# One store instead of two for the last rows, and a cast cut along another dimension, in a fused attention and mixer kernel

## The chip, the cores and the metric

The kernel runs on one core of one Trainium2 chip. The metric is the device time of one execution in microseconds. The core has five engines that run their own instruction streams: TensorE (PE in the profile, with its weight loads as PEld), VectorE (DVE), ScalarE, also called Activation (ACT), GpSimd (POOL) and SyncE (SP). Transfers between main memory (DRAM) and the on-chip memory (SBUF) are issued by SyncE, ScalarE or GpSimd, each on a queue of its own, and are carried out by 16 DMA engines that the queues share. PSUM is the memory that TensorE writes to.

## The reference

Inputs are q, k and v of shape (8 batches, 8 heads, 576 positions, 64), a matrix omega of 128 features, and four weight matrices of a mixer; all are float32, and so is the output of shape (8, 576, 512).

```python
def phi(x):                       # x = q or k, scaled by 64 ** -0.25
    h = x @ omega.T - sum(x * x) / 2
    return exp(h - max(h)) / sqrt(128)

kv  = einsum('bhsm,bhsd->bhmd', phi(k), v)
num = einsum('bhsm,bhmd->bhsd', phi(q), kv)
den = einsum('bhsm,bhm->bhs', phi(q), sum over s of phi(k)) + 1e-6
x   = num / den, heads side by side          # (8, 576, 512)

h   = relu(x^T @ w_tok1) @ w_tok2            # mixes positions: 576 -> 256 -> 576
u   = x + h^T
out = u + relu(u @ w_ch1) @ w_ch2            # mixes channels: 512 -> 1536 -> 512
```

So there are two stages: a linear attention with random features, and a mixer whose last part, the channel mix, does most of the multiplications.

## The kernel before

The work is cut by batch. The 576 positions of a batch are split into 512 main rows (`SM`) and 64 tail rows (`ST`). For every batch the function `attention` (from line 518 on) projects q and k, takes exponentials, multiplies k's features with v, and divides; `token_mix` mixes positions; `channel_mix` mixes channels of the 512 main rows in four groups `j` of 128 rows. The 64 tail rows of two batches are put together into one tile of 128 rows (`token_tail`), so that the tail rows of all eight batches make four such tiles. They are handled at the very end as a ninth call, `channel_mix(B, ...)` with `c == B`: its group `j` holds batch `2 * j` in partitions 0 to 63 and batch `2 * j + 1` in partitions 64 to 127.

All of this is written as a list of jobs with an engine, an estimated cost, a key and dependencies. A planner in the kernel (`Planner.run`) goes through the list and emits the instructions of each engine in the order of the keys and of the times it estimates; the order on every engine is thus fixed when the kernel is built. Buffers come from rings (for example four tiles `o` for results, three `kT`).

Two places matter here.

**The last stores.** In `channel_mix`, each group `j` has twelve matmuls into a PSUM bank (line 892), an addition of the residual on VectorE into a tile `o` of 128 rows (line 901), and a store. For the last group of the ninth call (`last`, `c == B` and `j == 3`) the columns are cut into two pieces of 384 and 128, so that the addition and store of the first piece can go while the second piece is still being multiplied. The stores of the ninth call are on line 911: since the 128 rows belong to two batches, there are two stores for each tile or piece, one for each half of the partitions. For the groups 2 and 3 the second one is issued by ScalarE's queue, which has nothing else to do by then, and the first by SyncE. Main rows of the other batches are stored on line 908, one store of 128 rows each.

**The casts of q and k.** For the batches 2 to 7, q and k are first copied from DRAM to a scratch area in DRAM with a cast from float32 to float16 (`load_transposed`, lines 353, 358 and 364, issued by GpSimd), and then read back by a transposing transfer on SyncE's queue (line 374). q is one transfer of the whole batch. k is cast in three: two for the tail rows (`cast_tail`, line 364) and one for the main rows (`cast_main`, line 358), which lie in DRAM as 8 heads of 512 x 64 = 32768 elements, with the tail rows of each head between them. GpSimd then waits for the transposed k before it issues the load of v (line 380), and multiplies v with k's scale in between (line 671).

What sets the shape of the cast: source and destination are given in the same order, head by head, and each head's elements are contiguous on both sides. In the program the instruction of line 358 carries 8 x 2 x 16384 elements on both sides.

Of the kernel before, what the change touches and what calls it, by code (L numbers as in the profile page):

```python
# [177 lines left out]
def kernel(  # L178
# [12 lines left out]
    nc = tc.nc  # L191

    B, H, S, D = q.shape
# [4 lines left out]
    P = 128  # L198
    SM = 512
    ST = S - SM  # L200
# [5 lines left out]
    R = SM // 2  # L206
# [73 lines left out]
    scratch = {}  # L280
# [3 lines left out]
    src = {"q": q, "k": k}  # L284
# [16 lines left out]
    def dma(eng, key, wire, fn, deps=(), take=(), give=(), cost=None):  # L301
        cost = (0.75 if eng == "POOL" else 0.45) if cost is None else cost
        job = add(eng, cost, key, fn, deps, take, give, wire=wire)
        if eng == "POOL":
            job.after = issued[-1] if issued else None
            issued.append(job)
        return job
# [41 lines left out]
    def load_transposed(b, key, deps=()):  # L349
        casts = []  # L350
        for n, w in enumerate("qk"):
            def cast(w=w):
                nc.gpsimd.dma_start(
                    out=scratch[w, b].rearrange("(p r) e -> p (r e)", p=P),
                    in_=src[w][b].rearrange("h s d -> (h s d)").rearrange("(p f) -> p f", p=P),
                )
            def cast_main(w=w):
                nc.gpsimd.dma_start(
                    out=scratch[w, b][0 : H * R].rearrange("(p r) e -> p (r e)", p=P),
                    in_=src[w][b, :, 0:SM, :].rearrange("h s d -> h (s d)").rearrange("h (c f) -> h c f", c=P // H),  # L360
                )
            def cast_tail(w=w):
                for g in range(2):
                    nc.gpsimd.dma_start(
                        out=scratch[w, b][H * R : H * RA, g * D : (g + 1) * D],
                        in_=src[w][b, 4 * g : 4 * g + 4, SM:S, :],
                    )
            if w == "k":
                casts.append(dma("POOL", key + 0.01 * n - 0.005, 0.8, cast_tail, deps, cost=1.1))
            casts.append(dma("POOL", key + 0.01 * n, 3.2, cast if w == "q" else cast_main, deps, cost=0.55))  # L370
        for n, w in enumerate("qk"):
            def back(w=w):
                t = (t_qT if w == "q" else t_kT)[place(w + "T", b)]
                nc.sync.dma_start_transpose(out=t.unsqueeze(1), in_=scratch[w, b])
            ld[w + "T", b] = dma("SP", key + 0.2 + 0.01 * n, 2.2, back, deps=casts, take=[(w + "T", b)], cost=2.5)
# [50 lines left out]
    def pads():  # L426
# [6 lines left out]
        out=w1m.rearrange("p j t -> p (j t)"), in_=moe_w_tok1[0:SM, :].rearrange("(p j) t -> p (j t)", j=NJ)))  # L433
# [23 lines left out]
    for i in range(2):  # L457
        c0 = i * (NCB // 2)
        j_wc2.append(dma("POOL", -3.0 + 0.1 * i, 3.85, lambda c0=c0: nc.gpsimd.dma_start(
            out=wc2[:, c0 : c0 + NCB // 2, :], in_=moe_w_ch2[c0 * P : (c0 + NCB // 2) * P, :].rearrange("(i p) d -> p i d", p=P))))  # L460
# [3 lines left out]
        out=omega16.rearrange("p (i d) -> p i d", i=2), in0=omega_nat.unsqueeze(1).broadcast_to((P, 2, D)), scalar1=c_scale, scalar2=None, op0=ALU.mult), deps=j_om)  # L464
    j_omt = add("PE", 0.06, -9.0, lambda: nc.tensor.transpose(bank16("om")[:, 0:P], omega16, ident16),
                deps=[j_om16, j_ident], take=[("bank", "om")])
# [378 lines left out]
    def channel_mix(c, key, jt):  # L845
        def moving(db):
            return (t_uT[place("uT", c)] if c < B else uTt)[:, :, db, :]
        jr = []
        for cb in range(NCB):
            n = ("h3", c, cb)  # L850
            def c1(cb=cb, n=n):
                ps = bank(n)
                for db in range(ND):
                    nc.tensor.matmul(ps, wc1[:, db, cb * P : (cb + 1) * P], moving(db), start=(db == 0), stop=(db == ND - 1))  # L854
            first = [tr[x] for x in tr if c < NPE and x[1] == c]
            if c == 0 and cb < 2:

                def c1a(cb=cb, n=n):
                    for db in range(ND - 1):
                        nc.tensor.matmul(bank(n), wc1[:, db, cb * P : (cb + 1) * P], moving(db), start=(db == 0), stop=False)  # L860
                def c1b(cb=cb, n=n):
                    nc.tensor.matmul(bank(n), wc1[:, ND - 1, cb * P : (cb + 1) * P], moving(ND - 1), start=False, stop=True)
                ja = add("PE", mm(3, 512), -0.02 + 0.001 * cb, c1a, deps=[*jt[:-1], j_wc1[0], *first], take=[("bank", n), ("r3", c)])
                ja.heavy = True
                j1 = add("PE", mm(1, 512), -0.01 + 0.001 * cb, c1b, deps=[ja, jt[-1]], give=[("uT", c)])
            else:
                j1 = add("PE", mm(4, 512), key + 0.5 * cb / NCB, c1, deps=[*jt, j_wc1[cb // (NCB // 2)], *first], take=[("bank", n), ("r3", c)],
                       give=[("uT", c)] if c < B else [])
            j1.heavy = True
            on_act = c >= NPE or BY[("r0", "r1")[c]][cb] == "A"  # L870
            def relu(cb=cb, n=n, on_act=on_act):
                o = t_r3[place("r3", c)][:, cb, :]
                if on_act:
                    nc.scalar.activation(out=o, in_=bank(n), func=AF.Relu)  # L874
                else:
                    nc.vector.tensor_relu(out=o, in_=bank(n))
            jr.append(add("ACT" if on_act else "DVE", 0.5 if on_act else 0.69, key + 0.5 * cb / NCB, relu, deps=[j1], take=[("r3", c)], give=[("bank", n)]))
        for j in range(NJ):
            last = c == B and j == NJ - 1
            for hf in range(2 if last else 1):  # L880
                n = ("h4", c, j, hf)
                cols = (slice(0, 3 * P), slice(3 * P, DM))[hf] if last else slice(0, DM)
                prev = None
                for part in range(3):
                    def c2(j=j, part=part, n=n, cols=cols):
                        ps, r3 = bank(n), t_r3[place("r3", c)]
                        for cb in range(4 * part, 4 * part + 4):
                            if c == 0 and cb == NCB - 1:
                                for db in range(ND):
                                    nc.tensor.matmul(ps[:, db * P : (db + 1) * P], t_uT[place("uT", c)][:, j, db, :], ident16,  # L890
                                                     start=False, stop=False, skip_group_check=True)
                            nc.tensor.matmul(ps[:, cols], r3[:, cb, j * P : (j + 1) * P], wc2[:, cb, cols], start=(cb == 0), stop=(cb == NCB - 1))  # L892
                    prev = add("PE", mm(4, cols.stop - cols.start) + (mm(4, P) if c == 0 and part == 2 else 0.0), key + 0.5 + 0.5 * (3 * j + part) / 12 + 0.2 * hf, c2,
                               deps=[prev, *jr[4 * part : 4 * part + 4], *j_wc2], take=[("bank", n)], give=[("r3", c)] + ([("uT", c)] if c == 0 else []))
                k2 = key + 0.5 + 0.5 * (3 * j + 3) / 12
                def oadd(j=j, n=n, cols=cols):
                    if c == 0:
                        nc.vector.tensor_copy(out=t_o[place("o", (c, j))], in_=bank(n))
                        return
                    uu = t_u[place("u", c)][:, j, :] if c < B else ut[j]  # L900
                    nc.vector.tensor_tensor(out=t_o[place("o", (c, j))][:, cols], in0=uu[:, cols], in1=bank(n)[:, cols], op=ALU.add)  # L901
                jo = add("DVE", (0.55, 0.27)[hf] if last else 0.69, k2, oadd, deps=[prev], take=[("o", (c, j))], give=[("bank", n)] + ([("u", c)] if 0 < c < B else []))
                def store(j=j, cols=cols, last=last):
                    o = t_o[place("o", (c, j))]
                    if c < B:
                        rows = out[c, 0:SM, :]
                        rows = rows.rearrange("(p j) d -> p j d", j=NJ)[:, j, :] if c else rows[j * P : (j + 1) * P, :]
                        nc.sync.dma_start(out=rows, in_=o)
                    else:
                        for i in range(2):  # L910
                            (nc.scalar if j >= 2 and i else nc.sync).dma_start(out=out[2 * j + i, SM:S, cols], in_=o[i * ST : (i + 1) * ST, cols])
                dma("SP", k2, 0.65, store, deps=[jo], give=[("o", (c, j))], cost=0.4 if c < B else 0.8)

    for i in range(4):
        transposes(0, "k", 2 * i, 2 * i + 2, HEAD["kx"][i], BY["kx"][i] == "A", HEAD["kxo"][i])
# [60 lines left out]
```

## Time and profile before

The median of three runs is 291.0 us (290.1 to 295.1). The profiled execution has a span of 287.5 us.

| What | Value |
|---|---|
| busy time of TensorE | 280.0 us, 97% of the span |
| busy time of ScalarE, VectorE, GpSimd | 153.8, 152.3, 93.7 us |
| matmuls of line 892 and line 854 (the channel mix) | 101.5 and 89.5 us of busy records, which overlap |
| stores of line 911, from issue to landing | 2.3 to 2.8 us |
| casts of k's main rows (line 358), from issue to landing | 8.9 to 18.7 us, median 10.8 |
| casts of q (line 353), from issue to landing | 6.0 to 15.5 us, median 6.7 |
| transposes of q and of k (line 374), time that the issue holds SyncE | 4.5 to 9.0 and 2.2 to 3.5 us |
| last matmul ends, last addition ends | 283.2 and 283.6 us |

How to read it: a busy time is the sum over an engine's instructions, and idle time of an engine that does not bound the kernel costs nothing. In the page's second part the span is cut into 40 equal slices, one digit each: 9 is 90% busy or more. "SPq" and "ACTq" are the DMA issues of SyncE and ScalarE, which have their own rows: a duration there is how long the issue held the engine's queue, and "to landing" runs from the start of the issue to the moment when all of the data have arrived. In rows of the form "a<-b xN" b is read and a is written, N times; numbers like 467/547/587 are the smallest, the median and the largest duration in nanoseconds.

### The profile page before, as it was taken

To read this page: it belongs to the slowest core of one execution; us is meant where nothing else is said; L and a number is where in the kernel's file an instruction comes from. 1 tells how busy PE (TensorE), PEld (TensorE's weight loads), DVE (VectorE), ACT (ScalarE), POOL (GpSimd) and SP (SyncE) were. 2 spreads that over 40 slices of the span, in tenths; PEclk is the share of its full clock that TensorE was granted. 3 is DMA by queue.
4 is the path that set the end of the run, shared out by engine and by line. 5 is a ranking of instruction groups with operands and counts; after the bars stand their busy time and mean duration, and the time that the engine had idled before them with its cause. 6 is when DMAs were issued, how large, how long until landed. Compare 5 with 4: busy or idle time off the path is not lost.

```text
span 287.5 us, 5598 instructions
## 1 busy us (share of the span) xinstructions
PE 280.0 (97%) x2186; PEld 141.3 (49%) x2186; DVE 152.3 (53%) x330; ACT 153.8 (53%) x322; POOL 93.7 (33%) x126
## 2 busy tenths in 40 slices
PE   7999989999999999999999999999999999999993
PEld 4585554445544544464445544554455444444442
DVE  4986963556659624774678346834766331032012
ACT  3994872098439554774666646663675402602600
POOL 8994950148015701660256014801230000000000
PEclk9999999999999999999999999999999999999998
DMA  8999999999978999997699979997931043013014
GB/s 194 194 194 195 202 210 107 208 225 172 136 122 196 148 91 200 166 213 125 110 200 168 137 126 172 178 160 117 196 74 39 0 104 115 2 37 127 2 36 110
DMA packets 85145, 39.59 MB, mean 138 GB/s; under 512 B 64480, under 2 KB 80224, under 8 KB 84832
## 3 DMA queue, kind: packets, MB, share of 16 engines
q0 software_dynamic: 33712, 17.45, 44.1%
q1 hardware_dynamic: 50624, 21.01, 38.6%
q10 hardware_dynamic: 784, 0.79, 0.9%
q8 instruction: 17, 0.28, 0.4%
q14 instruction: 8, 0.07, 0.1%
HBM read 35.88 MB, written 16.52 MB: 182 GB/s over the span
## 4 chain that ended last, share of the span: by engine, by line
PE 88%; DMA 5%; DVE 3%; POOL 2%; issue 0%; ACT 0%; SPq 0%; DVEq 0%; POOLq 0%
PE bank L892 33%; PE bank L854 30%; PE bank L776 4%; PE bank L759 4%; DMA r<-in_k_dram 3%; PE bank L638 3%; PE bank L652 2%; PE bank L720 2%; PE bank L684 2%; DMA wc<-in_k_dram 2%; POOL vs L671 1%; DVE km L664 1%; PE bank L760 1%; PE bank L835 1%; PE bank L485 1%; PE bank L722 1%
## 5 line engine op out<-in xcount | busy, mean ns | idle before, releaser
L874 ACT ACTIVATE r<-bank 128x512 f16<-128x512 f32 x106 | 63.6, 609 | 71.8 <-PE bank L854 71.2
L892 PE MATMUL bank<-wc,r 128*128 128x512 f16 (+2 forms) x444 | 101.5, 374 | 0.0
L854 PE MATMUL bank<-uT,wc 128*128 128x512 f16 x376 | 89.5, 379 | 0.1
L892 PEld LDWEIGHTS <-r 128*128 128x128 f16 x444 | 40.6, 98 | 47.8 <-issue 4.7
L854 PEld LDWEIGHTS <-wc 128*128 128x128 f16 x424 | 39.7, 98 | 42.4 <-issue 0.4
L664 DVE TENSOR_REDUCE km<-kp 128x8 f16<-128x1024 f16 x32 | 38.6, 1206 | 7.9 <-ACT kp L514 7.9
L514 ACT ACTIVATE qp<-bank 128x512 f16<-128x512 f32 x64 | 35.9, 650 | 10.1 <-PE bank L652 10.1
L671 POOL TENSOR_TENSOR vs<-v,vs 128x512 f16<-128x512 f16 x32 | 33.5, 1060 | 15.4 <-DVE vs L666 5.9
L514 ACT ACTIVATE kp<-bank 128x512 f16<-128x512 f32 x64 | 34.6, 641 | 5.9 <-PE bank L638 5.9
L730 DVE TENSOR_TENSOR x<-bank,rc 128x320 f16<-128x320 f32 x62 | 30.5, 492 | 2.1
L901 DVE TENSOR_TENSOR o<-u,bank 128x512 f32<-128x512 f16 x28 | 19.1, 681 | 19.4 <-PE bank L892 19.2
L380 POOL COPY junk<-kT 128x1 f16<-128x1 f16 x6 | 1.1, 187 | 65.0 <-DMA kT<-k 65.0
L779 DVE TENSOR_TENSOR u<-x,bank 128x512 f16<-128x512 f16 x28 | 17.4, 682 | 7.9 <-PE bank L776 7.9
L729 DVE RECIPROCAL rc<-bank 128x5 f32<-128x5 f32 x62 | 11.4, 184 | 14.4 <-PE bank L722 14.2
L767 DVE TENSOR_SCALAR r<-bank 128x512 f16<-128x512 f32 x7 | 4.8, 692 | 24.2 <-PE bank L760 24.2
L720 PEld LDWEIGHTS <-qp 128*128 128x128 f16 x256 | 12.7, 98 | 5.6 <-issue 0.4
L596 POOL TENSOR_TENSOR vbd<-vt,vbd 128x512 f16<-128x512 f16 (+1 forms) x7 | 8.2, 1175 | 20.3 <-issue 9.4
L759 PE MATMUL bank<-x,w1m 128*128 128x512 f16 x56 | 14.4, 379 | 0.0
L720 PE MATMUL bank<-kvsb,qp 128*128 128x65 f16 x256 | 14.0, 193 | 0.0
L684 PE MATMUL bank<-vs,kp 128*128 128x65 f16 x256 | 13.0, 193 | 0.8 <-POOL vs L671 0.8
L684 PEld LDWEIGHTS <-kp 128*128 128x128 f16 x256 | 10.9, 98 | 5.3 <-issue 1.5
L776 PE MATMUL bank<-r,w 128*128 128x512 f16 x56 | 13.4, 380 | 0.0
(109 smaller groups left out, 270.2 us busy)
## 6 DMA issues: line engine op xcount, KB each, us to landing
out_dram<-o SPq DMA_DIRECT2D x32, 256.0 KB, 3.2
q<-in_q_dram POOLq DMA_DIRECT2D x6, 576.0 KB, 6.7
wc<-in_moe_w_ch_dram POOLq DMA_DIRECT2D x4, 768.0 KB, 10.8
k<-in_k_dram POOLq DMA_DIRECT2D x6, 512.0 KB, 10.8
v<-in_v_dram POOLq DMA_DIRECT2D x6, 512.0 KB, 6.7
r<-in_q_dram POOLq DMA_DIRECT2D x4, 256.0 KB, 7.5
v<-in_v_dram POOLq DMA_DIRECT2D x4, 256.0 KB, 7.5
out_dram<-o SPq DMA_DIRECT2D x5, 128.0 KB, 2.4
```

Of the source, the lines that this page charges most:

```text
L514: nc.scalar.activation(out=out, in_=in_, func=AF.Exp, bias=0.0, scale=1.0)
L664: nc.vector.reduce_max(out=mx, in_=kpv, axis=AX.X)
L671: nc.gpsimd.tensor_tensor(out=vs[:, :, 0:D], in0=t_v[place("v", b)][:, hh[0] : hh[0] + 2, :].rearrange("p h (j d) -> p (h j) d", d=D), in1 ...
L684: nc.tensor.matmul(ps[:, i, :], kpv[:, 2 * i + j // 2, j % 2, :], vs[:, i * NJ + j, 0 : D + 1], start=(i == 0 and j == 0), stop=False, ski ...
L720: nc.tensor.matmul(ps[:, k, j * 65 : (j + 1) * 65], st, s[:, i, 0 : D + 1], start=True, stop=True)
L730: nc.vector.tensor_tensor(out=t_x[place("x", b)][:, :, (2 * hp + hs[0]) * D : (2 * hp + hs[0] + n) * D].rearrange("p j (i d) -> p i j d", ...
L759: nc.tensor.matmul(ps, w1m[:, j, tb * P : (tb + 1) * P], x[:, j, :], start=(j == 0), stop=False)
L776: nc.tensor.matmul(ps, w2_of(tb, j), r1[:, tb, :], start=(tb == 0), stop=(tb == NT - 1))
L854: nc.tensor.matmul(ps, wc1[:, db, cb * P : (cb + 1) * P], moving(db), start=(db == 0), stop=(db == ND - 1))
L874: nc.scalar.activation(out=o, in_=bank(n), func=AF.Relu)
L892: nc.tensor.matmul(ps[:, cols], r3[:, cb, j * P : (j + 1) * P], wc2[:, cb, cols], start=(cb == 0), stop=(cb == NCB - 1))
L901: nc.vector.tensor_tensor(out=t_o[place("o", (c, j))][:, cols], in0=uu[:, cols], in1=bank(n)[:, cols], op=ALU.add)
```

## The change

Two edits.

First, a tile of the ninth call is stored by one transfer of all 128 rows, to both batches at once, in place of two of 64 rows. Only the last group's first piece (384 columns, the one whose columns start at 0) goes on ScalarE's queue; everything else is on SyncE's. This is for fewer issues, and so that the two pieces of the last group don't stand behind each other on one queue. There are five stores on line 910 now instead of ten on line 911.

Second, the cast of k's main rows gives its source and destination in another order of dimensions: each head's 32768 elements are cut into 16 parts of 2048, and the part is the outermost dimension, the head the second one. The instruction then carries 16 x 8 x 2048 elements on both sides. This is for 128 packets of 4 KB in place of 16 of 32 KB. The same elements go to the same places.

```diff
             def cast_main(w=w):
                 nc.gpsimd.dma_start(
-                    out=scratch[w, b][0 : H * R].rearrange("(p r) e -> p (r e)", p=P),
-                    in_=src[w][b, :, 0:SM, :].rearrange("h s d -> h (s d)").rearrange("h (c f) -> h c f", c=P // H),
+                    out=scratch[w, b][0 : H * R].rearrange("(h c r) e -> c h (r e)", h=H, c=P // H),
+                    in_=src[w][b, :, 0:SM, :].rearrange("h s d -> h (s d)").rearrange("h (c f) -> c h f", c=P // H),
                 )
...
                     else:
-                        for i in range(2):
-                            (nc.scalar if j >= 2 and i else nc.sync).dma_start(out=out[2 * j + i, SM:S, cols], in_=o[i * ST : (i + 1) * ST, cols])
-                dma("SP", k2, 0.65, store, deps=[jo], give=[("o", (c, j))], cost=0.4 if c < B else 0.8)
+                        (nc.scalar if last and not cols.start else nc.sync).dma_start(out=out[2 * j : 2 * j + 2, SM:S, cols], in_=o[:, cols])
+                dma("SP", k2, 0.65, store, deps=[jo], give=[("o", (c, j))], cost=0.4)
```

The order of the instructions on TensorE, VectorE, ScalarE and GpSimd stays as it was; what differs is the shape of six casts on GpSimd, three fewer issues on SyncE and two fewer on ScalarE at the end.

## The prediction

> **What bounds the kernel now.** I read the page's busy shares and slices first, then the chain that ended last, then the last stores by line, then GpSimd around the first cast.
>
> ```profile
> span 287.5 us, 5598 instructions
> PE 280.0 (97%) x2186; PEld 141.3 (49%) x2186; DVE 152.3 (53%) x330; ACT 153.8 (53%) x322; POOL 93.7 (33%) x126
> ...
> PE   7999989999999999999999999999999999999993
> ...
> DMA  8999999999978999997699979997931043013014
> ```
>
> TensorE has work in every slice but the first and the last. In the trace's matmul records I find only two gaps over 0.2 us after 14 us (0.69 us at 23.3, 0.77 us at 37.1), and none over 0.07 us from 40 us to 283.2 us. So between 40 and 283 us nothing done to a transfer can shorten the run, unless it was making TensorE wait, and it was not.
>
> ```profile
> 272.82 10.40 PE bank L892 x60
> 283.32 0.29 DVE o L901
> ```
>
> These last two pieces of the chain say when arithmetic ends: 283.6 us. The span is 287.5, so 3.9 us remain, and only stores are left in it. Seen by line, in the last stretch:
>
> ```profile
> L911 SPq DMA_DIRECT2D out_dram<-o x7: 467/547/587, 277.9 to 283.8; - x7
> L901 DVE TENSOR_TENSOR o<-ut,bank x5: 289/689/689, 277.2 to 283.3; 128x512 f32<-128x512 f16 x3, 128x384 f32<-128x384 f16 x1, 128x128 f32<-128x128 f16 x1
> L911 ACTq DMA_DIRECT2D out_dram<-o x3: 547/567/749, 282.6 to 284.1; - x3
> ...
> DMA to landing us min/median/max: 2.3/2.4/2.8
> ```
>
> Ten stores for five additions; each issue holds its queue about 0.55 us, and the last one starts at 284.1 on the Activation queue, half a microsecond after its data were ready, because it stands behind another issue. It lands about 2.3 us later, at 286.1 by its semaphore; 1.4 us of waits and the closing barrier end the span. This tail is the only place where the first edit can act, and here nothing hides it.
>
> For the second edit, GpSimd around the first of the six casts:
>
> ```profile
> 31.91 0.56 POOL L358 DMA_DIRECT2D k<-in_k_dram  x1 [0.23 <-DMA v<-in_v_dram]
> 32.48 1.94 POOL L596 TENSOR_TENSOR vbd<-vt,vbd 128x1024 f16<-128x1024 f16 x1
> 34.37 1.06 POOL L671 TENSOR_TENSOR vs<-v,vs 128x512 f16<-128x512 f16 x1
> 35.37 1.33 POOL L345 DMA_DIRECT2D vt<-in_v_dram  x2
> 36.71 3.09 POOL L671 TENSOR_TENSOR vs<-v,vs 128x512 f16<-128x512 f16 x3
> ```
>
> GpSimd is busy without a break from the cast to the multiplication that ends TensorE's 0.77 us gap at 37.1. A longer cast issue here is paid in full.
>
> [...]the instruction carries 8 x 2 x 16384 on both sides, its packets are 16 of 32 KB, and in the packet records never more than 8 are in flight together (one exception of 9 at an edge), in two rounds of 2.43 us. The q cast, 32 x 9216, has up to 16 in flight. No plain transfer of before on the Sync or Activation queue has a slowest dimension below 64[...].
>
> [...]
>
> [...]the 2 KB packets of the 64-row stores at 279 to 282 us took 148 ns in the median, those of the 128-row stores of line 908 took 84.
>
> **The change part by part.**
>
> Edit 1, the stores. Each group of 128 rows is now one instruction, in SBUF 128 rows, in DRAM 2 x 64 rows (the instruction carries the two shapes as 128 x 1 x 512 and 2 x 64 x 512). Removed: five issues of about 0.55 us. The last piece needs no queueing any more: its data are ready at 283.61 and Sync is free, so it starts at about 283.65 rather than 284.14. That is worth 0.5 us if the transfers stay as quick. No new wait stands in front of it: the semaphore it reuses belongs to a store that landed long before.
>
> [...]The slowest dimensions are 128 and 2; the largest common divisor up to 16 is 2. All five stores then run on the same two engines, each carrying 64 rows of each store, where before a store used 16 engines with 4 rows each. Costs per packet from the records of before, as spacing on one engine: 80 ns for 2 KB (they last 84 and overlap a little), about 63 ns for 1.5 KB (last 65), 26 ns for 512 B (last 27). Each engine's list: three stores of 64 x 80 ns = 5.12 us each, 15.4 us; 64 x 63 ns = 4.0 us; 64 x 26 ns = 1.7 us; together 21.1 us. The first packet comes at 279.1 us as before (1.2 us after the issue at 277.9). The next stores are issued at about 278.8, 282.65, 283.05 and 283.65, always before the engines have drained what came earlier, so the list runs without a gap: the last packet ends at 279.1 + 21.1 = 300.2. Then 0.24 us to its semaphore (285.87 to 286.11 before) and 1.43 us to the end of the span (286.11 to 287.54): 301.8, that is 14.3 us more than 287.5. The second queue doesn't help, as it feeds the same two engines.
>
> Bounds of the packet cost: [...]At the other end stand the 148 ns of the 64-row stores: if one engine alone were that slow, 1.85 times 21.1 us, 39 us. I take 80 ns[...].
>
> Edit 2, the cast. 16 x 8 x 2048 has 16 as its slowest dimension, so 16 engines with 8 packets of 4 KB each replace 8 engines with two of 32 KB. Per engine 8 x 0.31 us = 2.4 us (an eighth of 2.43 us each) in place of 4.9: it lands some 2.4 us sooner, six times. TensorE's unbroken stretch from 40 us on hides all of it; the transpose that reads k is moreover issued after the q transpose, which holds Sync 4.5 to 9.0 us. What can be lost is issue time on GpSimd: 560 ns for 16 packets, 853 ns for the 256 of a tail cast; 128 packets lie between, about 0.70. The added 0.14 us counts once, at 31.9 us, and nothing later, where TensorE has a stock of other work. Bounds 0 to 0.3 us.
>
> Sum: +14.3 + 0.1 = +14.4 us on a median of 291.0: **305.4 us**.
>
> **The rivals.**
>
> Two engines, but another pair for each store[...]. Then the stores don't queue behind each other; the last to end is the third: issued 282.65, packets from 283.8, 5.1 us, 288.9, and some sharing; with 1.7 us of ending 290.6 to 291, +3.3 us: about 294.3, within 2%. [...]6%.
>
> All 16 engines as before, the outcome on the other side. The SBUF side has 128 rows and could be cut along them. Then [...]the last issue is 0.5 us earlier and 0.1 us goes to GpSimd: 290.5, no change that can be measured, perhaps slightly faster. For it speaks that 128-row stores of line 908 do so; against it, that those have 128 on both sides, and the cast which stays on 8 engines though 16 would be possible. 8%.
>
> Two engines at the slow packet rate: 39 us in place of 21.1: about 323. The records speak against it. 6%.
>
> That GpSimd, the casts or the transposes become the bound I don't give a case of its own: TensorE's stretch would have to break, which needs several microseconds of lateness in loads that come earlier, not later.
>
> **How the numbers follow.** Queueing on the same two engines 80%, the others 6, 8 and 6. The likeliest is 305.4. Within it: [...]up to some 311 if packets or the sharing of the two queues cost a quarter more than 80 ns; with 1 us of scatter the range is 302 to 311, which leaves out the three rivals, just under 2 in 10 with the edges. Slower by over 2% means above 296.8: 80 + 6 = 86%. Within 2%: 6 + 8 less a small part, 13%. Faster by over 2% would need 285.2, below what arithmetic leaves: 1%.
>
> **What would show it.** If I am right: line 910's stores go up from 2.4 us to landing, to 7 us for the first and well over 10 for the later ones; the DMA share stands near 2 of 16 (one tenth) for twenty microseconds after TensorE has ended; the arithmetic still ends near 283.7; the chain's end is unchanged and the gap to the span is about 18 us. The k cast lands sooner by about 2 us and TensorE's gaps after 40 us stay nil. I am wrong if the stores land in under 3 us (16 engines) or the first and the later ones land in about equal 6 to 7 us (pairs that rotate). If the end of arithmetic itself moves by more than 0.5 us, edit 2 did more than I allow.

## The result and the profile after

The changed kernel takes 304.7 us in the median of four runs (304.66 to 307.06), where the kernel before takes 291.06: a ratio of 1.05, with a 95% interval of 1.0433 to 1.0567. The profiled execution has a span of 302.7 us instead of 287.5.

First the page of the changed kernel, the lines that answer to those of before: span, busy time of the engines, and in 40 slices TensorE's and the DMA engines' busy share.

```profile
span 302.7 us, 5590 instructions
PE 279.6 (92%) x2186; PEld 140.5 (46%) x2186; DVE 152.0 (50%) x330; ACT 153.7 (51%) x322; POOL 93.4 (31%) x126
...
PE   7999899999999999999999999999999999999300
...
DMA  8999999799895999999899959994103200300111
```

TensorE did the same work in the same time (279.6 us against 280.0). Two and a half slices at the end are new, and nothing is in them but a DMA share of one tenth. The chain that ended last says when arithmetic ends (start, duration, what):

```profile
272.46 10.40 PE bank L892 x60
...
282.96 0.29 DVE o L901
```

It ends at 283.2 us, 0.4 earlier than before. From there to the end of the span it was 3.9 us and is 19.4 now. The stores of line 910 after the change:

```profile
L910 SPq DMA_DIRECT2D out_dram<-o x4: 511/602/7050, 277.5 to 283.3; - x4
...
L910 ACTq DMA_DIRECT2D out_dram<-o x1: 1132/1132/1132, 282.9 to 282.9; - x1
```

Five issues in place of ten, and the last one starts at 283.3, as early as it can. But it holds Sync for 7.05 us (the largest of the three numbers; before, none of the last ten held a queue over 0.75). The same stretch, from 276 to 304 us, seen from the DMA engines, first before and then after: 40 slices of 0.7 us, the share of 16 engines that is busy, and the bytes moved.

```profile
DMA  0000589800089700000000000000000000000000
GB/s 0 0 0 0 129 196 211 202 12 0 0 181 347 220 1 0 0 0 12 12 0 0 0 0 0 0 0 0 0 0 0 0 0 0 0 0 0 0 0 0
```

```profile
DMA  0000111111111111111111111111111111110000
GB/s 0 0 0 0 23 35 29 29 41 53 50 50 53 50 50 53 51 51 51 51 48 51 48 51 51 51 51 51 53 47 53 53 53 43 44 30 0 0 0 12
```

Before, there are two bursts with up to nine tenths of the engines and 347 GB/s. After, it is one tenth (two of sixteen are 12.5%) without a pause for 22 us, and a flat 50 GB/s. In the packet records of the changed kernel two packets are in flight for nine tenths of that time, and three for nearly all the rest: a packet of 2 KB lasts 84 ns, and the next but one starts 80 ns after it. The semaphore records agree: each store of before adds to its semaphore in 16 steps; each of the changed kernel in one step about 1 us after its issue starts (for the last one when its long issue is over), and then in two more. They land at 285.7, 293.7, 296.0 (the one of ScalarE's queue), 299.8 and 301.3 us.

GpSimd around the first cast, after:

```profile
31.52 0.56 POOL L358 DMA_DIRECT2D k<-in_k_dram  x1 [0.23 <-DMA v<-in_v_dram]
32.09 1.94 POOL L596 TENSOR_TENSOR vbd<-vt,vbd 128x1024 f16<-128x1024 f16 x1
33.98 1.06 POOL L671 TENSOR_TENSOR vs<-v,vs 128x512 f16<-128x512 f16 x1
```

Issuing 128 packets costs what issuing 16 did, 0.56 us. The six casts land in 9.1 us in the median, where they took 10.8:

```profile
DMA to landing us min/median/max: 7.7/9.1/16.0
```

The packet records have 16 to 20 of their packets in flight at the most, where it was 8 to 10.

### The profile page after: what moved, and what is told of

It reads as the page before. It is cut to its first block, busy times and chain, and to the rows that moved or that the text cites. A ratio compares the mean times of both kernels' runs of the same rounds, so it can differ in the third digit from the quotient of the medians.

```text
span 302.7 us, 5590 instructions
## 1 busy us (share of the span) xinstructions
PE 279.6 (92%) x2186; PEld 140.5 (46%) x2186; DVE 152.0 (50%) x330; ACT 153.7 (51%) x322; POOL 93.4 (31%) x126
## 4 chain that ended last, share of the span: by engine, by line
PE 83%; DMA 4%; DVE 2%; POOL 2%; issue 0%; ACT 0%; SPq 0%; DVEq 0%; POOLq 0%
PE bank L892 32%; PE bank L854 29%; PE bank L776 4%; PE bank L759 4%; DMA r<-in_k_dram 2%; PE bank L638 2%; PE bank L652 2%; PE bank L720 2%; PE bank L684 2%; DMA wc<-in_k_dram 2%; POOL vs L671 1%; DVE km L664 1%; PE bank L760 1%; PE bank L835 1%; PE bank L485 1%; PE bank L722 1%
## 5 line engine op out<-in xcount | busy, mean ns | idle before, releaser
L901 DVE TENSOR_TENSOR o<-u,bank 128x512 f32<-128x512 f16 x28 | 19.1, 681 | 19.4 <-PE bank L892 19.2
L759 PE MATMUL bank<-x,w1m 128*128 128x512 f16 x56 | 14.4, 379 | 0.0
```

What stands on the lines that cost most here:

```text
L759: nc.tensor.matmul(ps, w1m[:, j, tb * P : (tb + 1) * P], x[:, j, :], start=(j == 0), stop=False)
```

## The experiments

"Tail" below is the time from the end of the last addition to the end of the span: 3.9 us before, 19.4 after. It leaves out what happens at the start, where the profiled executions differ by up to 0.8 us (in all runs but those with a gap told of below, the times of the same matmuls differ from those of the kernel before by a constant, to within 0.3 us, from 39 us on).

### Each edit by itself

The stores alone: the kernel before with this edit, and the planner's cost of a store as in the change:

```diff
-                        for i in range(2):
-                            (nc.scalar if j >= 2 and i else nc.sync).dma_start(out=out[2 * j + i, SM:S, cols], in_=o[i * ST : (i + 1) * ST, cols])
+                        (nc.scalar if last and not cols.start else nc.sync).dma_start(out=out[2 * j : 2 * j + 2, SM:S, cols], in_=o[:, cols])
```

> The kernel before with the five merged stores alone; the cast as before. If the stores are the whole cause: span about 302, the same as with both edits, arithmetic ends near 283.2 to 283.7. If the cast on 16 engines carries part of it (either way), this run differs from the changed kernel by that part: over 1 us would be a part of note.

Measured: 304.5 us, ratio 1.0486 (1.0448 to 1.0524); span 302.3, tail 19.4. The stores are the whole loss.

The cast alone: the kernel before with the new access patterns of line 358.

> The kernel before with the recut cast alone. My theory: 287.5 us of span within 0.4, since TensorE has no gap to close; k lands 2 us sooner and nothing takes that up. Rival: the cast shortens a wait (span 286 or less), or the 128 packets delay GpSimd at 32 us (span up to 0.3 us longer).

Measured: 289.79 against 290.20 us, ratio 0.9982 (0.9967 to 0.9998); span 287.0, no gap of TensorE after 40 us. The span lies 0.5 us below that of before, just outside the stated 0.4 us, and the starts alone differ by as much. The interval ends just short of 1, so the same kernel was timed again:

> The run of the cast alone once more, in more rounds, since its interval of 0.9967 to 0.9998 ended just short of 1. If the cast on 16 engines takes away short waits of TensorE that only some executions have (the slower cast showed that there is little room): a ratio near 0.998 again, below 1. If it was scatter of the start: 1.000 within 0.1%.

Measured: 289.76 against 290.19 us, ratio 0.9973 (0.9955 to 0.9990). So it does help, by 0.2 to 0.3%. The spread tells part of how: 22 runs with the new cast end between 289.2 and 290.5, 50 runs of the kernel before between 289.35 and 294.7. The long ones are gone. But the lower quartile falls too, from 289.8 to 289.5 us, and no profile shows where that comes from.

### How many engines

To vary the number of engines, the merged stores were pointed at 4 batches x 32 rows and at 8 batches x 16 rows: the same five instructions, number of rows and packet sizes. Only the places in DRAM change, of which a store now covers 4 or 8.

```diff
-                        (nc.scalar if last and not cols.start else nc.sync).dma_start(out=out[2 * j : 2 * j + 2, SM:S, cols], in_=o[:, cols])
+                        (nc.scalar if last and not cols.start else nc.sync).dma_start(out=out[4 * (j // 2) : 4 * (j // 2) + 4, SM + 32 * (j % 2) : SM + 32 * (j % 2) + 32, cols], in_=o[:, cols])
```

and for 8 x 16

```diff
+                        (nc.scalar if last and not cols.start else nc.sync).dma_start(out=out[:, SM + 16 * j : SM + 16 * j + 16, cols], in_=o[:, cols])
```

> The changed kernel, but each merged store goes to 4 batches x 32 rows in place of 2 x 64; every tail row is still written once, with the same packets, but with rows of other batches (the output is not the reference's). If the count of engines is the common divisor (4 now) and a packet still costs 80 ns: each engine's list halves, the third store's packets begin at 284, 5.4 us for what is left, span about 291 (3 us over before). [...]If it isn't the count of engines at all but that one store covers two DRAM blocks: about 302 or more.

> As the run with 4 x 32, but 8 batches x 16 rows (again rows of other batches in the output, each tail row written once). Divisor 8 at 80 ns per packet: after the third store's first packet at 283.5 there is 2.7 us of packets, span about 288 (0.4 us over before). [...]If the count of engines is not the cause: about 302 or more.

Measured: spans of 293.5 and 290.0 us (ratios 1.0216, 1.0157 to 1.0276, and 1.0037, 1.0020 to 1.0054). The stretch from 276 to 304 us, for 4 x 32 and then for 8 x 16:

```profile
DMA  0000222222222222222222000000000000000000
GB/s 0 0 0 12 23 12 59 79 102 99 102 102 94 67 83 85 95 92 90 94 94 89 24 0 0 0 12 0 0 0 0 0 0 0 0 0 0 0 0 0
```

```profile
DMA  0000043454205345510000000000000000000000
GB/s 0 0 0 0 0 61 35 173 196 187 97 15 56 88 180 201 177 33 0 0 0 12 0 0 0 0 0 0 0 0 0 0 0 0 0 0 0 0 0 0
```

They show two tenths and 100 GB/s, then four to five tenths and 200 GB/s, where two engines gave one tenth and 50. The semaphores count the same: 4 and 8 steps after the first. The tail is 10.5 us with 4 engines and 5.9 with 8.

| engines per merged store | 2 | 4 | 8 |
|---|---|---|---|
| tail, us | 19.4 | 10.5 | 5.9 |
| median duration of a 2 KB packet, ns | 84 | 84 | 84 |
| mean duration of a 2 KB packet, ns | 91 | 104 | 122 |
| packets of 2 KB over 100 ns, of 384 | 16 | 35 | 73 |

The spans are 2.5 and 2.0 us over my first figures of 291 and 288, and 8.5 and 12 us under the 302 of a cause other than the count of engines. The count follows the common divisor of the 128 rows and the places, 2, 4 and 8 in these three runs, and a store to 4 or 8 places in DRAM is faster than one to 2 (tails of 10.5 and 5.9 us against 19.4), so it isn't that more places cost more. The mean packet gets slower with more engines (91, 104 and 122 ns), but the usual one does not (84). The long packets come in bunches: in the first 2 to 3 us of the first store in all three runs, and with 4 and 8 engines once more between 284 and 287 us; in between, nearly all last 84 ns in all three. What makes the long ones slow stays open. (The span of 8 x 16 also has 0.8 us of a TensorE gap at 92 us, ahead of line 684, in it; the tail has not.)

### One queue

The changed kernel with the last tile's first piece on Sync too:

```diff
-                        (nc.scalar if last and not cols.start else nc.sync).dma_start(out=out[2 * j : 2 * j + 2, SM:S, cols], in_=o[:, cols])
+                        nc.sync.dma_start(out=out[2 * j : 2 * j + 2, SM:S, cols], in_=o[:, cols])
```

> The changed kernel with the first piece of the last tile on the Sync queue as well, all five merged stores on one queue. If two engines' packet time is all that counts: 302 to 303 us of span, as the changed kernel, as both queues feed the same two engines. If the second queue brings relief or is itself the delay (its first packet came 3.8 us after its issue): 1 us or more of difference.

Measured: 304.7 us (ratio 1.0491, 1.0431 to 1.0551), span 302.6, tail 19.4. The stores' issues:

```profile
L910 SPq DMA_DIRECT2D out_dram<-o x5: 511/687/4941, 277.5 to 287.5; - x5
```

The fourth and fifth hold Sync 4.6 and 4.9 us and the last starts only at 287.5, 4 us later than with two queues; the end is the same. Here, where the two engines were never idle, neither the second queue nor the issue 4 us earlier was worth anything: the tail is 19.4 us in both.

### One and two merged stores

The kernel before, with `j == 0` alone, and then `j < 2`, stored by one transfer each:

```diff
-                        for i in range(2):
-                            (nc.scalar if j >= 2 and i else nc.sync).dma_start(out=out[2 * j + i, SM:S, cols], in_=o[i * ST : (i + 1) * ST, cols])
+                        if j == 0:
+                            nc.sync.dma_start(out=out[2 * j : 2 * j + 2, SM:S, cols], in_=o[:, cols])
+                        else:
+                            for i in range(2):
+                                (nc.scalar if j >= 2 and i else nc.sync).dma_start(out=out[2 * j + i, SM:S, cols], in_=o[i * ST : (i + 1) * ST, cols])
```

> The kernel before with only the first of the last tiles (j = 0) stored by one transfer. Two-engine theory: its packets (64 per engine, 5.2 us) run from 278.8 to 284.0 while TensorE still multiplies, and are drained when the last stores come; from the end of the last addition to the end of the span 3.9 to 4.2 us, as before. If a merged store holds up what follows in some other way (its queue, its issue, the second DRAM block), the tail grows by a fifth of the whole loss, 3 us.

Measured: 292.6 us (ratio 1.0070, 1.0032 to 1.0108), span 289.8, tail 5.5. That is more than I expected, and less than the rival's 7. The waits of Sync from 276 us on (who waits for what, us, times, longest):

```profile
SPq L911 <- DVE o L901: 13.4, 1, 13.4
SPq L914 <- DVE o L901: 3.1, 2, 2.7
SPq L914 <- DMA out_dram<-o: 1.3, 1, 1.3
```

The third line doesn't stand in the kernel before: a store waits for a store. With nine transfers in the last group instead of ten, the last store reuses the semaphore of the merged one, eight transfers back. That one landed at 286.55 us only, and the last store was issued at 286.61, 1.3 us after its queue was free. (The issue ahead of it had itself held Sync for 1.27 us.) So this run has a wait that my edit made. But the wait is worth little: ScalarE's last store, which waited for no other, landed at 288.55 us, and the last store at 288.73. What my expectation had wrong is that the merged store would be drained at 284.0; it landed 2.2 us after the last addition (284.3), in part because its list starts slowly, as told below. ScalarE's last store has 14 of its 16 semaphore steps by 287.46 and the last two at 288.25 and 288.55: two engines are late.

> As the run with one merged store, but j = 0 and j = 1 merged, which keeps two engines busy to about 289.1. Theory: the later stores spread over 16 engines, but their share on these two waits behind the list: last packet about 289.8, from the last addition to the end 7.8 us in place of 3.9. If the engines were not shared by the later stores: 4 to 6 us (the second merged store alone would end near 289.1 plus 1.7). If other costs count, twice a fifth of the loss: 10 us.

Measured: 297.2 us (ratio 1.0231, 1.0161 to 1.0302), span 294.0, tail 10.8. There is no such wait here. The merged stores land at 285.6 and 292.1 us, and each of Sync's later stores has 14 of its 16 semaphore steps by 286.9 and the last two only at 291.6 to 292.8. The two late steps of 16 fit two engines that are the same for every store, on which ordinary stores of the queue stand behind the merged ones' list. My figure of 7.8 was too small by 3.0: I left out that list's slow start (below), and I had 0.7 us for the later stores' own rows on the two engines, 8 of each tile, which work out to 1.3. That makes about 2 us; some 1 us stays unexplained.

### The cast on fewer engines

The kernel before with the cast cut in 4 parts per head instead of 16:

```diff
-                    out=scratch[w, b][0 : H * R].rearrange("(p r) e -> p (r e)", p=P),
-                    in_=src[w][b, :, 0:SM, :].rearrange("h s d -> h (s d)").rearrange("h (c f) -> h c f", c=P // H),
+                    out=scratch[w, b][0 : H * R].rearrange("(h c r) e -> c h (r e)", h=H, c=4),
+                    in_=src[w][b, :, 0:SM, :].rearrange("h s d -> h (s d)").rearrange("h (c f) -> c h f", c=4),
```

> The kernel before with the cast of k cut as 4 x 8 x 8192, so that by the divisor only 4 engines carry it, 8 packets of 16 KB each, some 10 us in place of 5. The stores are those of before. Theory (the cast has slack, so neither 16 nor 4 engines change the time): 287.5 us of span within 0.5, k lands about 5 us later than before, TensorE without gaps after 40 us. Rival (the cast matters, and 16 engines gained the 0.2% that the run of the cast alone showed): gaps after 60 us and a span at least 1 us longer.

Measured: 313.2 us, ratio 1.0744 (1.0656 to 1.0832), span 311.8. My theory of slack fell. The packets are never more than 6 in flight (8 to 10 in the kernel before, 16 to 20 with the new cast: the casts' 4, 8 and 16 engines are read from these counts), and the six casts land in 16.3 us in the median in place of 10.8. As the packets are half as large as before, it isn't their size that makes the cast slow. TensorE's longest waits in this run, and below them those of the kernel before:

```profile
PE bank L652 <- DMA qT<-q: 7.3, 2, 4.3
PE bank L546 <- DMA kT<-k: 7.0, 3, 2.9
PE bank L684 <- POOL vs L671: 1.8, 3, 0.9
```

```profile
PE bank L943 <- DVE mask L423: 1.2, 1, 1.2
PE bank L684 <- POOL vs L671: 0.8, 1, 0.8
PE bank L505 <- DMA r<-in_k_dram: 0.7, 1, 0.7
```

TensorE now waits for the transposed q and k, which it never did. It waits for q too, although q's cast is as before. The likely reason is that the transposing transfers of q have to share engines with k's cast: with the cast on 4, 8 or 16 engines, the issue of q's transpose ends 0.8 to 2.6 us after the last packet of k's cast, in all six batches of each of the three runs. How long that issue holds Sync, with k's cast on 4 engines, on 8 (the kernel before has 4497/6714/8976), and on 16 (the cast alone):

```profile
L374 SPq DMA_TRANSPOSE qT<-q x6: 9259/11659/13930, 44.5 to 206.5; - x6
```

```profile
L374 SPq DMA_TRANSPOSE qT<-q x6: 3798/4694/6268, 44.1 to 185.7; - x6
```

So with 8 engines the loads were near the limit: 5 us later breaks TensorE's stretch in every batch. The waits for loads are only 15 of the 24 us that the span has grown by. In four of the gaps, those of 2.75 us and more, the granted clock falls to one half, 2.0 to 2.9 us after the gap begins, and stays there for 3.4 to 6.8 us; the gaps of 1.34 us and less don't show this. TensorE is busy for 288.7 us in place of 280.0 for the same work, which is most of the rest. The granted clock in 40 slices:

```profile
PEclk9999999999979997799959999999899999999999
```

Two of the other runs with the old cast show the beginning of such gaps; this is TensorE in the run with one merged store:

```profile
PE bank L652 <- DMA qT<-q: 0.8, 1, 0.8
```

It is a gap at 112 us. The run with the third queue alone, told next, has one of 0.16 us at the same place. With the new cast no run shows a wait for q there. That the long executions of before come from such gaps is a guess, as none of those was profiled; and the new cast doesn't end all gaps: the one of 8 x 16 at 92 us, a wait for GpSimd's product of v (line 671), is with the new cast.

### A version without the loss

The stores of before, with the half microsecond at the last issue taken away: the third tile's second half goes on GpSimd's queue, so that ScalarE's is free for the last tile. With the new cast and without it:

```diff
-                            (nc.scalar if j >= 2 and i else nc.sync).dma_start(out=out[2 * j + i, SM:S, cols], in_=o[i * ST : (i + 1) * ST, cols])
+                            (nc.gpsimd if j == 2 and i else nc.scalar if j == 3 and i else nc.sync).dma_start(out=out[2 * j + i, SM:S, cols], in_=o[i * ST : (i + 1) * ST, cols])
```

> The recut cast, and the stores of before with one change: the second half of the third tile goes on GpSimd's queue, so that the last tile's second halves find ScalarE's queue free. If the last issue standing behind another (284.1 in place of 283.65) is worth what it seems: the last landing 0.4 us sooner, from the last addition to the end 3.5 us in place of 3.9; with the cast's 0.2% a ratio of 0.997 to 0.998. If GpSimd's store takes long to land and ends last: 4 us or more, ratio 0.998 to 1.000.

> The kernel before with that third queue alone, the cast as before. 3.5 us from the last addition to the end, ratio 0.9985; the interval will hardly leave 1. If the third queue does nothing: ratio 1.000 within 0.1%.

Measured: 0.9984 (0.9964 to 1.0005) with the cast, 0.9994 (0.9962 to 1.0026) without; tails of 4.4 us in both. The last issues do start earlier, 0.25 us after the last addition instead of 0.5, but the tail is longer, not shorter (3.9 us before, 4.0 and 3.9 with the new cast alone). The store on GpSimd's queue goes in 32 packets of 4 KB that last 0.16 to 0.41 us, where ScalarE's went in 64 packets of 2 KB, most of them of 0.084 us; its last data come 1.9 to 2.0 us after the last addition, 1.3 before. Beside it the last piece's first packet comes 1.6 us after its issue instead of 1.3, and its packets are spread over 0.7 us (0.45 before). That the one causes the other is likely, but not shown apart. One of the 22 runs with the new cast took 292.9 us. The version to keep is the new cast with the stores of before: 289.76 us, 0.9973 of the kernel before.

## Why the prediction was right

It gave 305.4 us and a mechanism, two engines for all merged stores; measured are 304.7 and that mechanism. The first merged store lands 8.1 us after its issue and the others 13 to 18, as the prediction's signs said. That the numbers are so close is in part luck: the tail was worked out as 18.2 us (283.6 to 301.8) and is 19.4, while the median of three runs to which the difference was added, 291.0, is 0.8 us above that of 50 later runs, 290.2. Step by step:

- **Arithmetic's end as the floor.** 283.2 us against 283.6; TensorE without gaps after 40 us. Right.
- **How many engines, and the same ones.** Both were assumptions for these stores: the trace of before has no store with fewer than 64 outermost. Stores of 128 rows to 2, 4 and 8 places ran on two, four and eight engines, by the semaphore (2, 4 and 8 steps after the first) and by the DMA share (one tenth, two, four to five). The trace of before showed such a count only for a cast on GpSimd's queue, and there less sharply than I wrote: the casts of k, 8 x 2 x 16384, have 9 or 10 packets in flight for up to 0.15 us in four of six batches and never more than 8 otherwise, those of q up to 19. That all merged stores share the same two engines is inferred from two packets in flight throughout, from landings up to 18 us after the issue, and from the two late steps of the ordinary stores with two merged ones. Which two, the records don't say. That they are the same is what tells the 14 us from the 3 us of my first rival.
- **The packet cost.** 80 ns for 2 KB on each of two engines is 51 GB/s, and that is the plateau. That the merged stores' packets would go at the 84 ns of the 128-row stores and not at the 148 of the 64-row ones was my estimate; their median is 84. The list took 22.2 us (278.81 to 301.01) against 21.1 worked out. It lost 1.4 us at its start, where 15 of the 48 packets up to 282 us last 0.13 to 0.41 us instead of 0.084, and won 0.3 us at its end, where packets of 1.5 KB and 512 B took 61 and 24 ns instead of 63 and 26. Then 0.33 us to the semaphore and 1.35 us to the end: 278.81 + 22.20 + 0.33 + 1.35 = 302.69. The end of before was split wrongly: 286.1 us is the landing of ScalarE's first piece, and the last store landed at 286.44. From its last data at 285.87 it is 0.57 us to the semaphore and 1.10 us to the end; the sum of 1.67 us, which is all that was used, is right.
- **The second queue doesn't help.** Shown by the run with one queue: 19.4 us of tail with one queue as with two. The trace of before doesn't show that two queues slow each other: SyncE's packets took 165 ns in the median from 284.0 us to ScalarE's first one at 284.38, and the 64 of ScalarE's that followed took 84 in the median. In the changed kernel, from 286.67 us on, two packets of one queue and two of the other start in turn, as two engines that alternate between the queues would give.
- **An earlier last issue is worth 0.5 us.** Not shown. With stores on 16 engines, where it could count, it brought nothing, but there a slower store on GpSimd's queue came with it.
- **The cast.** "TensorE's unbroken stretch from 40 us on hides all of it" held for the two profiled runs of the cast alone, but the new cast took away 0.2 to 0.3% of the median, where I had put down a loss of 0.1 us. It lands 1.7 us sooner in the median, not 2.4. The 0.14 us of longer issue did not exist: 0.55 to 0.56 us for 16 as for 128 packets. And "several microseconds of lateness" that would break the stretch were nearer than I thought: the case that I set aside, loads that become the bound, is what a cast on 4 engines makes true, with 5.5 us of lateness in the median.

The medians differ by 13.7 us, the spans by 15.2; the kernel before was measured at 290.2 to 290.3 in the later comparisons, which puts the difference at 14.4.

## What to carry to other kernels

Before merging two transfers into one, look at the outermost dimension of both access patterns as the instruction carries them: here stores with 2, 4 and 8 there on DRAM's side ran on 2, 4 and 8 of the 16 engines, although SBUF's side had 128 rows in all three. A slow transfer was harmless here only as long as something hid it: at the end of the kernel nothing did, and 14 us were lost; in mid-kernel a cast on 8 engines in place of 16 cost 0.2 to 0.3%, and one on 4 engines 7%. And a stretch in which an engine is never idle says that earlier loads can't help much; it does not say how late they may become: that takes a run with a slower one.

## What the runs showed of the hardware that I had not expected

- With three merged stores on two engines still undone, the next issue on the same queue held it for 7.05 us; with all five on one queue, the fourth and fifth held it for 4.6 and 4.9 us, against 0.5 to 0.7 for the first three.
- The first packets of the piece on ScalarE's queue started 3.8 us after its issue (282.86 to 286.67), and 2.8 us with 8 engines, against 1.7 before. The second queue's store got its turn only after a while, though the packets of the two queues take turns from 286.67 us on.
- The first store on two engines ran at 100 ns per 2 KB packet instead of 80. Long packets of 0.13 to 0.41 us stand among its first 48, and longer ones (up to 0.94 us) at the same place with 4 and 8 engines; the median is 84 ns in all three.
- In gaps of TensorE of 2.75 us and more, in the run with the cast on 4 engines, the granted clock fell to one half for 3.4 to 6.8 us; in gaps of 1.34 us and less it did not.
